# Gated MLP behind attention and a soft mixture: four plain turns become six Strassen turns, and float64 weights are made float32 in three operations in place of four

## The chip, the cores and the metric

The kernel runs on one core of one Trainium2 chip. The metric is the device time of one execution in microseconds. Each execution is the whole chain below, from the inputs in device memory to the output in device memory.

## The reference

Three layers follow each other. The first is a decayed linear attention over 4 batches, 8 heads, 768 positions and 64 channels. The second is a soft mixture of 8 experts with 4 slots each. The third, which the change is about, is a gated MLP over 3072 tokens:

```
h = x @ w_in                                  # x 3072x512, w_in 512x2048
g = h * (1.0 / (1.0 + np.exp(-1.702 * h)))
return (g @ w_out).astype(np.float32)         # w_out 2048x512
```

`w_in` and `w_out` reach the kernel as float64 (a float32 array times a numpy double). The kernel sees them as pairs of 32-bit words and has to put together the float32 value of each number itself, from the sign, exponent and upper mantissa in the upper word and three mantissa bits in the lower one.

## The kernel before

**Stages.** In order of time: attention in 32 steps (some 0 to 143 us), the experts, whose weights stream in through the SP queue (to 184 us), a short passage in which the slot outputs are turned into the matrix `W2s`, and then the MLP. In the MLP the output of the mixture is not written out: `h` comes straight from `W2s` and the transposed token weights `cT` with one product of depth 128.

**Plain turns.** The tokens are cut into four groups of 768 (`tg`), the 2048 hidden columns into 16 blocks of 128 (`f`). A plain turn `j` is one pair (`tg`, `f`): `do_h(j)` makes the 768 values of `g` for the block (`h_mm`, two products of 384 columns, then `h_gate` on ScalarE), splits them into a rounded upper part `GHI` (`h_hi`, ScalarE) and a rest `GLO` (`h_lo`, VectorE), and `do_out(j)` runs 18 products of 128x512: six blocks of 128 tokens, each as GHI with whi, GHI with wlo, GLO with whi. The work `do_h(j)` is issued in the middle of turn `j-2`, in front of its tenth product. One group (`WHOLE = 2`) goes through all 16 blocks in plain turns. The other three go through the first few only: `HF` = 4 blocks, and for the last of them `LAST_HF` = 8.

**Strassen turns.** What is left of the three groups is done in Strassen turns: 256 tokens against a pair of blocks (`p`, 256 hidden columns), with seven products in place of eight. A turn is 21 products of 128x256 and the two of 256 columns that make `h` (`s_h`). There are nine groups of such turns, one for each 256 tokens; their results are put together on VectorE (`ev_a` to `ev_d`) during the next group's first turns, and added to the rows in device memory.

**The weights.** The 27 late pieces of the weights (15 rows of `w_out`, 12 pieces of `w_in`) are loaded during the plain turns into three buffers (`f64`, `NST`), converted, and split. `LATE_IN` and `LATE_OUT` say at which `do_h` a piece is converted, and at the next one a row of `w_out` is split into `whi` and `wlo` (`split_hi` on ScalarE, `split_lo` on VectorE). `ROUNDS` operations of a conversion stand ahead of `h_lo` on VectorE, the rest behind it. `w2_a`, `w2_b` and `w2_c` extend `W2s` by 512 columns three times; they stand in given turns of the plain part. For the Strassen turns `make_sums`, `make_his` and `make_lows` make the sums of weight blocks for pair `p` in the turn that `PAIR_AT` gives and the one after it. Ten smaller pieces (`EARLY`) are converted during attention, with their last two operations on GpSimd.

**Order.** The order on each engine is that of the program text; nothing is moved by a scheduler. Each engine's queue runs in order.

Of the kernel before, what the change touches and what calls it, by code (L numbers as in the profile page):

```python
# [17 lines left out]
def attention_moe_gelu_kernel(  # L18
# [38 lines left out]
    TG = 2 * HS  # L57
    HF = 4

    LATE_IN = {1: (2, 4, 5, 6), 2: (9, 11, 13, 14), 3: (15, 16, 17, 18)}  # L60
    LATE_OUT = {4: 7, 5: 8, 6: 10, 7: 12, 8: 19, 9: 20, 10: 21, 11: 22, 12: 24, 13: 25, 14: 27, 15: 28}
    PAIR_AT = {2: 18, 3: 21, 4: 24, 5: 26, 6: 28, 7: 29}
    LAST_HF = 8
    ROUNDS = 3
    NST = 3
    F64_MIN = 2.0 ** -15 * 1.125
    CB = 256

    const = ctx.enter_context(tc.tile_pool(name="const", bufs=1, side="left"))
# [116 lines left out]
    def conversion(key, out, guard):  # L186
# [13 lines left out]
        yield  # L200
        if guard is DVE:
            DVE.scalar_tensor_tensor(out=out, in0=m, scalar=F64_MIN, in1=a.bitcast(F32),
                                     op0=ALU.is_ge, op1=ALU.mult)
        else:
            POOL.tensor_scalar(out=m, in0=m, scalar1=F64_MIN, scalar2=None, op0=ALU.is_ge)
            POOL.tensor_tensor(out=out, in0=a.bitcast(F32), in1=m, op=ALU.mult)

    def by_turns(*work, rounds=9):

        work = list(work)  # L210
        while work and rounds:
            work = [w for w in work if next(w, 0) is None]
            rounds -= 1
        return work
# [17 lines left out]
    def do_early(c):  # L232
        o = EARLY[c][-1]
        convert_abs(("early", c), o)
        by_turns(conversion(("early", c), o, POOL))


    S_a = [attn.tile([P, P], F32, tag=f"sa{i}", name=f"sa{i}", bufs=1) for i in range(4)]
# [244 lines left out]
    with tc.manual_schedule():  # L483
# [299 lines left out]
        def convert_early(f):  # L783
            convert_abs(("out", f))
            wo[f] = wo_ring[f]
            return conversion(("out", f), wo[f], DVE)

        def split_hi(f):
            ACT.activation(out=whi[f], in_=wo[f], func=AF.Copy)
# [89 lines left out]
        def convert_late(j, rounds=9):  # L879
            work = []  # L880
            for key in turns.get(j, ()):
                if key[0] == "out":
                    o = wo[key[1]] = wo_ring[key[1] % 10]
                else:
                    o = w_in_sb[key[1]][:, key[2], :]
                if key not in magn:
                    convert_abs(key)
                work.append(conversion(key, o, DVE))
            return by_turns(*work, rounds=rounds)

        def finish_late(j, work):
# [149 lines left out]
        def w2_rest():  # L1041
# [2 lines left out]
            rest0[:] = convert_late(0, ROUNDS)  # L1044


        extra = {(0, 3): w2_rest, (0, 6): lambda: do_h(1), (0, 13): lambda: do_h(2),
                 (7, 4): lambda: w2_a(1, "xt"), (9, 4): lambda: w2_b(1, "xt"), (9, 8): lambda: w2_c(1),
                 (15, 4): lambda: w2_a(2, "xt"), (16, 4): lambda: w2_b(2, "xt"), (16, 8): lambda: w2_c(2),
                 (19, 4): lambda: w2_a(3, "xt"), (20, 4): lambda: w2_b(3, "xt"), (20, 8): lambda: w2_c(3)}  # L1050

        def both(x, y):
            return lambda: (x(), y())
# [255 lines left out]
        for j in range(NJ):  # L1309
            at = {n: work for (jj, n), work in extra.items() if jj == j}  # L1310
            if 0 < j < NJ - AHEAD:
                at[9] = lambda: ahead(j + AHEAD)
                if j in (9, 16, 20):

                    at[9], at[12] = lambda: h_mm(j + AHEAD, (1,)), at[9]
            do_out(j, at)
# [39 lines left out]
```

## Time and profile before

| | |
|---|---|
| time, median of 3 runs | 479.23 us (478.05 to 479.63) |
| profiled execution, its own time | 478.11 us |
| its span, first to last instruction | 476.1 us |
| granted TensorE clock, mean | 1.000 |
| TensorE busy | 465.3 us, 98% |
| VectorE busy | 375.5 us, 79% |
| ScalarE busy | 303.3 us, 64% |
| GpSimd busy | 76.5 us, 16% |

The span is 2.0 us shorter than the execution's own time. Busy shares are means over stages that differ. In the rows further down PE is TensorE's matmuls, PEld its weight loads, DVE VectorE, ACT ScalarE, POOL GpSimd, SPq the queue of SP that issues most transfers.

### The profile page before, as it was taken

The page shows a single profiled execution, that of the slowest core. Times are in us where ns is not written, and L with a number is a line of the kernel's source. Part 1 is how long each engine was busy: PE and PEld are TensorE (multiplying, and loading weights), DVE is VectorE, ACT ScalarE, POOL GpSimd, SP SyncE. Part 2 cuts the span into 40 slices and gives each one's busy share as a digit, 9 for nine tenths or more (in the row PEclk, how much of TensorE's full clock was granted, in tenths as well). Part 3 has the DMA queues.
Part 4 walks back from the last instruction along what each step waited for, and adds up shares of the span by engine and source line. Part 5 has one row for each costly group of instructions (what it writes and reads, how often), then busy time and mean ns, then how long its engine had stood idle before and what let it go on. Part 6 is the DMA issues. An engine that isn't in the chain of part 4 may idle for free.

```text
span 476.1 us, 10660 instructions
## 1 busy us (share of the span) xinstructions
PE 465.3 (98%) x3991; PEld 388.0 (81%) x3991; DVE 375.5 (79%) x903; ACT 303.3 (64%) x605; POOL 76.5 (16%) x125
## 2 busy tenths in 40 slices
PE   7999999999999999999999999999999999999996
PEld 4887887888876444787888778888899999999996
DVE  5777988988875344897787689998779989888885
ACT  5877777777854155876865877566665655655551
POOL 3534434434311100000000000000001111011101
PEclk9999999999999999999999999999999999999999
DMA  7999999999999996465643532100313332133024
GB/s 186 259 283 285 269 297 270 276 302 289 290 335 387 410 407 252 131 222 178 219 133 108 202 133 89 44 0 2 133 46 45 45 45 29 18 45 45 9 38 89
DMA packets 81796, 81.52 MB, mean 171 GB/s; under 512 B 54736, under 2 KB 63440, under 8 KB 81744
## 3 DMA queue, kind: packets, MB, share of 16 engines
q1 hardware_dynamic: 79296, 76.63, 51.3%
q0 software_dynamic: 2304, 4.20, 6.4%
q8 instruction: 32, 0.52, 0.5%
q14 instruction: 20, 0.16, 0.1%
q10 hardware_dynamic: 144, 0.00, 0.0%
HBM read 69.80 MB, written 11.01 MB: 170 GB/s over the span
## 4 chain that ended last, share of the span: by engine, by line
PE 81%; DMA 10%; DVE 5%; SPq 1%; ACT 1%; issue 1%; DVEq 0%; ACTq 0%
PE bo L1014 26%; PE bp L1180 24%; DMA w<-in_moe_w_dram 7%; PE bs L301 4%; PE bx L348 3%; PE bx L340 3%; DMA k<-in_k_dram 2%; PE bsh L1136 2%; PE bq L263 2%; PE bst L314 2%; PE bhh L967 2%; PE bt L359 2%; PE bk L265 2%; PE bl L369 1%; PE bp L441 1%; SPq L128 1%
## 5 line engine op out<-in xcount | busy, mean ns | idle before, releaser
L1014 PE MATMUL bo<-wlo,GHI 128*128 128x512 f32 x192 | 75.3, 395 | 0.1
L1150 ACT ACTIVATE GHI<-G_all 128x896 fp32r<-128x896 f32 x48 | 45.9, 955 | 46.1 <-DVE G_all L1143 45.9
L1014 PE MATMUL bo<-whi,GLO 128*128 128x512 f32 x192 | 75.1, 394 | 0.0
L1014 PE MATMUL bo<-whi,GHI 128*128 128x512 f32 x192 | 74.8, 393 | 0.1
L1143 DVE TENSOR_TENSOR G_all<-G_all 128x128 f32<-128x128 f32 x192 | 47.4, 288 | 18.5 <-ACT G_all L1139 15.9
L1210 POOL DMA_DIRECT2D out_dram<-f x16 | 14.3, 1048 | 279.5 <-DVE G_all L1143 264.9
L1180 PE MATMUL bp<-tc,GHI 128*128 128x256 f32 x288 | 55.9, 282 | 0.0
L1155 DVE TENSOR_TENSOR GLO<-G_all,GHI 128x896 fp32r<-128x896 f32 x48 | 52.1, 1085 | 0.0
L975 ACT ACTIVATE G_all<-bhh 128x384 f32<-128x384 f32 x64 | 28.2, 490 | 34.4 <-PE bhh L967 34.3
L1180 PE MATMUL bp<-whi,GHI 128*128 128x256 f32 x192 | 49.5, 281 | 0.0
L1180 PE MATMUL bp<-wlo,GHI 128*128 128x256 f32 x192 | 49.2, 282 | 0.0
L1180 PE MATMUL bp<-whi,GLO 128*128 128x256 f32 x168 | 47.5, 283 | 0.0
L1180 PEld LDWEIGHTS bp<-tc,GHI 128*128 128x128 f32 x288 | 44.4, 190 | 0.0
L1014 PEld LDWEIGHTS bo<-wlo,GHI 128*128 128x128 f32 x192 | 36.0, 188 | 9.6 <-issue 2.5
L1014 PEld LDWEIGHTS bo<-whi,GLO 128*128 128x128 f32 x192 | 36.0, 188 | 7.8 <-DVE GLO L981 0.3
L1014 PEld LDWEIGHTS bo<-whi,GHI 128*128 128x128 f32 x192 | 36.1, 188 | 7.5 <-DVE W2s L921 0.5
L1180 PE MATMUL bp<-tc,GLO 128*128 128x256 f32 x144 | 40.4, 280 | 0.0
L981 DVE TENSOR_TENSOR GLO<-G_all,GHI 128x768 fp32r<-128x768 f32 x32 | 30.6, 955 | 10.4 <-ACT GHI L978 10.2
L282 POOL TENSOR_TENSOR qdT<-qT,qtab 128x384 f32<-128x384 f32 x32 | 32.4, 1012 | 39.7 <-PE bx L340 16.7
L273 ACT ACTIVATE qT<-bq 128x384 f32<-128x384 f32 x32 | 22.6, 707 | 20.1 <-PE bq L263 18.4
L1180 PEld LDWEIGHTS bp<-wlo,GHI 128*128 128x128 f32 x192 | 34.7, 189 | 0.0
L1180 PEld LDWEIGHTS bp<-whi,GHI 128*128 128x128 f32 x192 | 34.6, 189 | 0.0
(231 smaller groups left out, 1040.2 us busy)
## 6 DMA issues: line engine op xcount, KB each, us to landing
w<-in_moe_w_dram SPq DMA_DIRECT2D x64, 512.0 KB, 6.7
f<-in_moe_w_out_dram SPq DMA_DIRECT2D x15, 512.0 KB, 3.3
qr<-in_q_dram SPq DMA_DIRECT2D x32, 192.0 KB, 4.2
k<-in_k_dram SPq DMA_DIRECT2D x64, 96.0 KB, 4.8
v<-in_v_dram SPq DMA_DIRECT2D x64, 96.0 KB, 4.1
f<-in_moe_w_in_dram SPq DMA_DIRECT2D x12, 512.0 KB, 3.8
out_dram<-o SPq DMA_DIRECT2D x24, 256.0 KB, 2.3
out_dram<-f POOLq DMA_DIRECT2D x16, 256.0 KB, 4.7
```

The lines of the kernel that those rows point to most:

```text
L273: ACT.activation(out=t.rearrange("m (p c) -> m c p", c=R), in_=bq[:, :HS].rearrange("m (c p) -> m c p", c=R), func=AF.Copy)
L282: POOL.tensor_tensor(out=qdT[s], in0=qT[s].rearrange("m (c i) -> m c i", c=R), in1=qtab[:, hp, None, :].to_broadcast([P, R, P]), op=ALU.mult)
L301: PE.matmul(bs[h][:, cs], kT[s][hs, cs], qT[s][hs, cs], start=True, stop=True)
L340: PE.matmul(bx[:, c * P:(c + 1) * P], state(s, first + c), qdT[s][:, c, :], start=(c == chunks[0]), stop=False)
L975: ACT.activation(out=g[j][:, u * HS:(u + 1) * HS], in_=bh[j][u][:, :HS], func=AF.Gelu_apprx_sigmoid)
L981: DVE.tensor_tensor(out=glo[j][:, o], in0=g[j][:, o], in1=ghi[j][:, o].bitcast(F32), op=ALU.subtract)
L1014: PE.matmul(ob[t], a[j][:, t * P:(t + 1) * P], w[f], start=(begin and i == 0), stop=(end and i == 2))
L1143: DVE.tensor_tensor(out=o, in0=x, in1=y, op=op)
L1150: ACT.activation(out=sh[j], in_=gs(j)[:, P:], func=AF.Copy)
L1155: DVE.tensor_tensor(out=sl[j], in0=gs(j)[:, P:], in1=sh[j].bitcast(F32), op=ALU.subtract)
L1180: PE.matmul(bank_of(gi, i)[1], x, w, start=begin, stop=end)
L1210: POOL.dma_start(out=rows_of(gi, k), in_=cells[:, C11 + 2 * k:C11 + 2 * k + 2], accum_op=ALU.add)
```

## The change

`LAST_HF` goes from 8 to 4, so that the last group, too, leaves plain turns after four blocks: 28 plain turns and 54 Strassen turns in place of 32 and 48. The tables that place the conversions, the sums and the `w2_` steps are written anew for 28 turns. A conversion loses its fourth operation, the guard that made tiny numbers zero. ScalarE, which took the absolute value of the upper word as it is, now multiplies it by 2^-112 as well, which puts the exponent in float32's place and lets tiny numbers become zero there; VectorE's first operation shifts ScalarE's result in place of the raw word. For the early pieces both GpSimd operations go.

```
-    LATE_OUT = {4: 7, 5: 8, 6: 10, 7: 12, 8: 19, 9: 20, 10: 21, 11: 22, 12: 24, 13: 25, 14: 27, 15: 28}
+    LATE_OUT = {4: 8, 5: 10, 6: 11, 7: 13, 8: 16, 9: 17, 10: 18, 11: 20, 12: 21, 13: 22, 14: 23, 15: 24}
...
-    LAST_HF = 8
-    ROUNDS = 3
+    LAST_HF = 4
+    ROUNDS = 2
...
-        ACT.activation(out=m, in_=staged[key][:, :, 1].bitcast(F32), func=AF.Abs)
+        ACT.activation(out=m, in_=staged[key][:, :, 1].bitcast(F32), func=AF.Abs, scale=F64_TO_32)
...
-        a = out.bitcast(U32) if key[0] != "early" else stage[key[1] % 2][:, 2 * CB:3 * CB]
-        DVE.tensor_scalar(out=a, in0=up, scalar1=3, scalar2=0x3FFFFFFF,
-                          op0=ALU.logical_shift_left, op1=ALU.bitwise_and)
+        a = m.bitcast(U32)
+        DVE.tensor_scalar(out=a, in0=a, scalar1=3, scalar2=None, op0=ALU.logical_shift_left)
         yield
-        DVE.scalar_tensor_tensor(out=a, in0=up, scalar=0xC0000000, in1=a,
+        DVE.scalar_tensor_tensor(out=a, in0=up, scalar=0x80000000, in1=a,
                                  op0=ALU.bitwise_and, op1=ALU.bitwise_or)
         yield
-        DVE.scalar_tensor_tensor(out=a, in0=low, scalar=29, in1=a,
+        DVE.scalar_tensor_tensor(out=out.bitcast(U32), in0=low, scalar=29, in1=a,
                                  op0=ALU.logical_shift_right, op1=ALU.bitwise_or)
-        yield
-        if guard is DVE:
-            DVE.scalar_tensor_tensor(out=out, in0=m, scalar=F64_MIN, in1=a.bitcast(F32),
-                                     op0=ALU.is_ge, op1=ALU.mult)
-        else:
-            POOL.tensor_scalar(out=m, in0=m, scalar1=F64_MIN, scalar2=None, op0=ALU.is_ge)
-            POOL.tensor_tensor(out=out, in0=a.bitcast(F32), in1=m, op=ALU.mult)
```

The rows below are the order of instructions on VectorE, line and operation, output from input, and size. First the passage from the experts to the MLP, in the kernel before; `wor` is a row of `w_out`, `f` the buffer with its float64, `cvm` ScalarE's absolute value, `W2s` the correction of the first columns of `W2s`, `wlo` a `split_lo`.

```order
L912 COPY soT<-bso 128x128 x2
L192 TENSOR_SCALAR wor_3153<-f_3156 128x512
L195 SCALAR_TENSOR_TENSOR wor_3153<-f_3156,wor_3153 128x512
L921 TENSOR_TENSOR W2s<-bw,W2s 64x128
L198 SCALAR_TENSOR_TENSOR wor_3153<-f_3156,wor_3153 128x512
L202 SCALAR_TENSOR_TENSOR wor_3153<-cvm,wor_3153 128x512
L921 TENSOR_TENSOR W2s<-bw,W2s 64x128
L792 TENSOR_TENSOR wlo_3302<-wor_3153,whi_3287 128x512
L981 TENSOR_TENSOR GLO<-G_all,GHI 128x768
```

The same place in the changed kernel:

```order
L905 COPY soT<-bso 128x128 x2
L193 TENSOR_SCALAR cvm<-cvm 128x512
L195 SCALAR_TENSOR_TENSOR cvm<-f_3136,cvm 128x512
L914 TENSOR_TENSOR W2s<-bw,W2s 64x128
L198 SCALAR_TENSOR_TENSOR wor_3133<-f_3136,cvm 128x512
L914 TENSOR_TENSOR W2s<-bw,W2s 64x128
L785 TENSOR_TENSOR wlo_3282<-wor_3133,whi_3267 128x512
L974 TENSOR_TENSOR GLO<-G_all,GHI 128x768
```

The two operations ahead of the first `W2s` row now read `cvm`, where they read the float64 buffer, and the row L202 is gone.

The second place is the turn in which the sums for the first pair (`sp`, `wos`) are made. Before, this is turn 18, with one conversion in it:

```order
L1095 TENSOR_TENSOR sp<-sp 128x256
L1095 TENSOR_TENSOR sp<-wos_3321,sp 128x256
L1095 TENSOR_TENSOR wos_3321<-wos_3321,sp 128x256
L1095 TENSOR_TENSOR wos_3321<-wos_3321 128x256
L192 TENSOR_SCALAR wos_3325<-f_3156 128x512
L195 SCALAR_TENSOR_TENSOR wos_3325<-f_3156,wos_3325 128x512
L198 SCALAR_TENSOR_TENSOR wos_3325<-f_3156,wos_3325 128x512
L981 TENSOR_TENSOR GLO<-G_all,GHI 128x768
L792 TENSOR_TENSOR wlo_3309<-wos_3324,whi_3294 128x512
L202 SCALAR_TENSOR_TENSOR wos_3325<-cvm,wos_3325 128x512
```

In the changed kernel it is turn 15:

```order
L1089 TENSOR_TENSOR sp<-sp 128x256
L1089 TENSOR_TENSOR sp<-wos_3301,sp 128x256
L1089 TENSOR_TENSOR wos_3301<-wos_3301,sp 128x256
L1089 TENSOR_TENSOR wos_3301<-wos_3301 128x256
L193 TENSOR_SCALAR cvm<-cvm 128x512 x2
L195 SCALAR_TENSOR_TENSOR cvm<-f_3136,cvm 128x512 x2
L974 TENSOR_TENSOR GLO<-G_all,GHI 128x768
L785 TENSOR_TENSOR wlo_3289<-wos_3304,whi_3274 128x512
L198 SCALAR_TENSOR_TENSOR wos_3305<-f_3136,cvm 128x512
L198 SCALAR_TENSOR_TENSOR w_in_3313<-f_3136,cvm 128x512
```

Two conversions stand there now, two operations of each ahead of `GLO` and one of each behind it.

## Rows read from the trace of the kernel before

**Rows 1.** Busy time by stage: stretch, length, PE, PEld, DVE, ACT, POOL, clock, DMA share.

```profile
core 0: us, PE busy (x) PEld busy (x) DVE busy (x) ACT busy (x) POOL busy (x), PEclk, DMA share, GB/s
20.00:184.00 164.00, 160.84 (x2001) 118.66 (x1997) 118.71 (x360) 108.62 (x266) 52.31 (x74) 1.00 1.02 318
206.00:330.00 124.00, 124.00 (x561) 99.98 (x560) 104.46 (x179) 85.75 (x164) 0.00 (x0) 1.00 0.37 124
345.00:462.00 117.00, 117.00 (x988) 117.00 (x987) 100.82 (x245) 67.47 (x95) 12.50 (x14) 1.00 0.25 38
```

**Rows 2.** Timeline of PE, the products `h_mm` (start, duration, engine, line).

```profile
221.33 0.51 PE L967 MATMUL bhh<-cT,W2s 128*128 128x384 f32 x2
...
227.03 0.51 PE L967 MATMUL bhh<-cT,W2s 128*128 128x384 f32 x2
...
241.08 0.51 PE L967 MATMUL bhh<-cT,W2s 128*128 128x384 f32 x2
...
307.34 0.51 PE L967 MATMUL bhh<-cT,W2s 128*128 128x384 f32 x2
...
329.77 0.51 PE L967 MATMUL bhh<-cT,W2s 128*128 128x384 f32 x2
```

**Rows 3.** The chain that ended last, Strassen turns, the first and last of 44.

```profile
342.55 2.50 PE bp L1180 x21
...
459.99 2.51 PE bp L1180 x21
```

**Rows 4.** Timeline of DVE, passage to the MLP (idle time before an instruction in brackets).

```profile
187.16 0.43 DVE L192 TENSOR_SCALAR wor<-f 128x512 uint32<-128x512 uint32 x1
187.62 0.69 DVE L195 SCALAR_TENSOR_TENSOR wor<-f,wor 128x512 uint32<-128x512 uint32 x1
188.46 0.29 DVE L921 TENSOR_TENSOR W2s<-bw,W2s 64x128 fp32r<-64x128 f32 x1
```

**Rows 5.** Timeline of ACT, the same place.

```profile
187.35 0.69 ACT L183 ACTIVATE cvm<-f 128x512 f32<-128x512 f32 x1
```

**Rows 6.** Timeline of PE, the same place.

```profile
188.81 0.62 PE L967 MATMUL bhh<-cT,W2s 128*128 128x384 f32 x2
189.26 1.89 PE L926 MATMUL bw<-w_in,soT 128*128 128x256 f32 x8
190.80 1.52 PE L1014 MATMUL bo<-whi,GHI 128*128 128x512 f32 x5
```

**Rows 7.** Timeline of PEld, turns 1 and 2.

```profile
196.68 0.19 PEld L1014 LDWEIGHTS bo<-whi,GLO 128*128 128x128 f32 x1 [0.27 <-DVE GLO L981]
...
201.34 0.19 PEld L1014 LDWEIGHTS bo<-wlo,GHI 128*128 128x128 f32 x1 [0.53 <-DVE wlo L792]
```

**Rows 8.** Timeline of DVE in the later plain turns.

```profile
290.50 0.76 DVE L921 TENSOR_TENSOR W2s<-w2raw,W2s 64x128 fp32r<-64x128 f32 x2
...
295.17 0.42 DVE L1095 TENSOR_TENSOR wos<-wos 128x256 f32<-128x256 f32 x1
...
296.88 0.95 DVE L981 TENSOR_TENSOR GLO<-G_all,GHI 128x768 fp32r<-128x768 f32 x1
297.75 0.68 DVE L792 TENSOR_TENSOR wlo<-wor,whi 128x512 fp32r<-128x512 f32 x1
298.35 0.75 DVE L1105 TENSOR_TENSOR whi<-wos,whi 128x256 fp32r<-128x256 f32 x2
...
299.69 0.42 DVE L192 TENSOR_SCALAR wor<-f 128x512 uint32<-128x512 uint32 x1
...
301.49 0.95 DVE L981 TENSOR_TENSOR GLO<-G_all,GHI 128x768 fp32r<-128x768 f32 x1
...
309.50 0.96 DVE L981 TENSOR_TENSOR GLO<-G_all,GHI 128x768 fp32r<-128x768 f32 x1 [0.60 <-ACT GHI L978]
```

**Rows 9.** Timeline, an early conversion: DVE's first operation, and ACT's.

```profile
28.47 0.29 DVE L192 TENSOR_SCALAR stage<-stage 128x256 uint32<-128x256 uint32 x1
...
29.53 0.43 ACT L183 ACTIVATE w_in<-stage 128x256 f32<-128x256 f32 x1
```

**Rows 10.** Waits of SP's queue: line, releaser, us in total, times, longest.

```profile
SPq L229 <- DVE stage L198: 1.7, 3, 0.9
```

More of the change, by code (lines that the diff above doesn't have):

```diff
@@ L58, in attention_moe_gelu_kernel @@
     HF = 4
-    LATE_IN = {1: (2, 4, 5, 6), 2: (9, 11, 13, 14), 3: (15, 16, 17, 18)}
-    LATE_OUT = {4: 7, 5: 8, 6: 10, 7: 12, 8: 19, 9: 20, 10: 21, 11: 22, 12: 24, 13: 25, 14: 27, 15: 28}
-    PAIR_AT = {2: 18, 3: 21, 4: 24, 5: 26, 6: 28, 7: 29}
-    LAST_HF = 8
-    ROUNDS = 3
+    LATE_IN = {1: (2, 4, 5, 6), 2: (7, 9, 11, 12), 3: (14, 15, 17, 19)}
+    LATE_OUT = {4: 8, 5: 10, 6: 11, 7: 13, 8: 16, 9: 17, 10: 18, 11: 20, 12: 21, 13: 22, 14: 23, 15: 24}
+    W2_AT = {1: (9, 11), 2: (14, 16), 3: (19, 21)}
+    PAIR_AT = {2: 15, 3: 17, 4: 19, 5: 21, 6: 23, 7: 25}
+    LAST_HF = 4
+    ROUNDS = 2
     NST = 3
-    F64_MIN = 2.0 ** -15 * 1.125
+    F64_TO_32 = 2.0 ** -112
     CB = 256
@@ L182, in convert_abs, with conversion @@
         m = mask
-        ACT.activation(out=m, in_=staged[key][:, :, 1].bitcast(F32), func=AF.Abs)
+        ACT.activation(out=m, in_=staged[key][:, :, 1].bitcast(F32), func=AF.Abs, scale=F64_TO_32)
         magn[key] = m
-    def conversion(key, out, guard):
+    def conversion(key, out):
         t, m = staged.pop(key), magn.pop(key)
         up, low = t[:, :, 1], t[:, :, 0]
-        a = out.bitcast(U32) if key[0] != "early" else stage[key[1] % 2][:, 2 * CB:3 * CB]
-        DVE.tensor_scalar(out=a, in0=up, scalar1=3, scalar2=0x3FFFFFFF,
-                          op0=ALU.logical_shift_left, op1=ALU.bitwise_and)
+        a = m.bitcast(U32)
+        DVE.tensor_scalar(out=a, in0=a, scalar1=3, scalar2=None, op0=ALU.logical_shift_left)
         yield
-        DVE.scalar_tensor_tensor(out=a, in0=up, scalar=0xC0000000, in1=a,
+        DVE.scalar_tensor_tensor(out=a, in0=up, scalar=0x80000000, in1=a,
                                  op0=ALU.bitwise_and, op1=ALU.bitwise_or)
         yield
-        DVE.scalar_tensor_tensor(out=a, in0=low, scalar=29, in1=a,
+        DVE.scalar_tensor_tensor(out=out.bitcast(U32), in0=low, scalar=29, in1=a,
                                  op0=ALU.logical_shift_right, op1=ALU.bitwise_or)
-        yield
-        if guard is DVE:
-            DVE.scalar_tensor_tensor(out=out, in0=m, scalar=F64_MIN, in1=a.bitcast(F32),
-                                     op0=ALU.is_ge, op1=ALU.mult)
-        else:
-            POOL.tensor_scalar(out=m, in0=m, scalar1=F64_MIN, scalar2=None, op0=ALU.is_ge)
-            POOL.tensor_tensor(out=out, in0=a.bitcast(F32), in1=m, op=ALU.mult)
     def by_turns(*work, rounds=9):
@@ L234, in do_early @@
         convert_abs(("early", c), o)
-        by_turns(conversion(("early", c), o, POOL))
+        by_turns(conversion(("early", c), o))
     S_a = [attn.tile([P, P], F32, tag=f"sa{i}", name=f"sa{i}", bufs=1) for i in range(4)]
@@ L785, in convert_early @@
             wo[f] = wo_ring[f]
-            return conversion(("out", f), wo[f], DVE)
+            return conversion(("out", f), wo[f])
         def split_hi(f):
@@ L887, in convert_late @@
                     convert_abs(key)
-                work.append(conversion(key, o, DVE))
+                work.append(conversion(key, o))
             return by_turns(*work, rounds=rounds)
@@ L1044, in w2_rest @@
             rest0[:] = convert_late(0, ROUNDS)
[L1047 to L1050, printed above, removed]
+        extra = {(0, 3): w2_rest, (0, 6): lambda: do_h(1), (0, 13): lambda: do_h(2)}
+        for n, (ja, jb) in W2_AT.items():
+            extra[ja, 4] = lambda n=n: w2_a(n, "xt")
+            extra[jb, 4] = lambda n=n: w2_b(n, "xt")
+            extra[jb, 8] = lambda n=n: w2_c(n)
         def both(x, y):
@@ L1312, in attention_moe_gelu_kernel @@
                 at[9] = lambda: ahead(j + AHEAD)
-                if j in (9, 16, 20):
+                if j in [jb for ja, jb in W2_AT.values()]:
                     at[9], at[12] = lambda: h_mm(j + AHEAD, (1,)), at[9]
```

## The prediction

> **What bounds the kernel now.** I read the busy time by stage first, then the timeline of TensorE's products, then the waits. From 20 to 184 us the transfers are the limit: the DMA share is 1.02 of a possible 1, with VectorE and GpSimd far from full [rows 1]. TensorE shows as busy there too, but a product that waits for its weights counts as busy, so that figure alone decides nothing. From 206 us on it is the other way round: the DMA share falls to 0.37 and 0.25, and TensorE is busy for 124.00 of 124.00 us and for 117.00 of 117.00 us, at a granted clock of 1.00, the higher level of 2.4 GHz [rows 1]. The reader should see that these two stretches are regular as well as full: plain turns follow each other at one distance, Strassen turns at another [rows 2, 3]. So in the MLP time is TensorE's turns. The only places where another engine holds it are the passage into the MLP and turns 1 and 2 [rows 6, 7].
>
> **The exchange of turns.** The products `h_mm` at 307.34 and 329.77 are five plain turns apart: 22.43 / 5 = 4.486 us a turn [rows 2]. The four turns that go are the last group's blocks 4 to 7, ordinary ones, so 4 x 4.486 = 17.94 us go. The first and the last of the 44 Strassen turns on the chain are 43 turns apart: 117.44 / 43 = 2.731 us a turn, evictions of the group before included [rows 3]. Six more cost 16.39 us. The exchange gives **-1.55 us**. The bounds are narrow, 0.2 us either way, because both distances are those of turns in which nothing but TensorE was late. VectorE has 100.82 us of work in 117.00 us there [rows 1], and the new groups of six turns leave it more room for the same evictions than groups of four did.
>
> A rule can be set beside this. The Trainium skill, "TensorE: Matmul & The Clock Gate", section "Back-to-back issue gap", lists 518 cycles for 512 columns and 262 for 256 at 2.4 GHz. With 390 for 384 columns, my estimate from that page's pattern, a plain turn would be 18 x 518 + 2 x 390 = 10,104 cycles or 4.21 us, a Strassen turn 23 x 262 = 6,026 cycles or 2.51 us, and the exchange -1.77 us. The trace has both turns longer, by 0.28 and 0.22 us, so the measured -1.55 stands in the sum.
>
> **The first conversion of the MLP.** Before, VectorE's first two operations on row 1 of `w_out` began at 187.16 straight from the raw words and were out of the way when the correction of `W2s` was due at 188.46 [rows 4]. Now they need ScalarE's `cvm`, which runs from 187.35 and ends at 188.04 [rows 5]. Queued behind them on VectorE is that correction, and TensorE waits for it: `h_mm(0)` starts at 188.81, right behind it, then the 256-column piece of `W2s`, and only then the first product of turn 0 at 190.80 [rows 6]. The two operations take 0.46 (187.16 to 187.62) and at most 0.69 us, so the correction starts at 188.04 + 0.46 + 0.69 = 189.19 in place of 188.46. That is **+0.7 us** for everything behind it. The bounds are 0 (if ScalarE got to `cvm` earlier than the row says) and 0.75.
>
> **What the shorter conversions give back.** In turns 1 and 2 weight loads sat idle 0.27 us for `GLO` and 0.53 us for a `wlo` [rows 7]. Each of these stands behind conversions on VectorE. One operation of 0.69 us less ahead of the first, and two less ahead of the second, outweigh the 0.7 us by which all of it starts later, so both waits should go. A weight load runs ahead of its product, so TensorE lost less than these 0.80 us. I take half, **-0.4 us**, with bounds 0 and -0.8.
>
> **VectorE in turns 15 to 22.** Here the change packs work closer, and this is the edit I cost at nothing that needs its cover named. In these eight turns stand nine conversions, eight `GLO`, seven `split_lo`, four sets of sums, four of lows, one `w2_a` and two corrections of `W2s`. By distances between starts [rows 8]: three operations of a conversion 1.80 (299.69 to 301.49), `GLO` 0.87, a split 0.60, sums 1.71, lows 1.34; the `w2_a` operation as a split 0.60; a pair of corrections 0.76. The sum is 16.2 + 7.0 + 4.2 + 6.8 + 5.4 + 0.6 + 1.5 = 41.7 us. TensorE needs 8 x 4.486 = 35.9 us for the turns, and 1.21 more for `w2_a` (221.33 to 227.03) and some 0.6 each for two `w2_b` (227.03 to 241.08 less three turns) [rows 2]: 38.3 us. VectorE falls 3.4 us behind. What covers it is the lead of two turns: `GLO` can start 2.16 us after `h_mm` (307.34 to 309.50 [rows 2, 8]), and is wanted at the third product two turns later, 2 x 4.486 - 7 x 0.23 = 7.36 us after `h_mm`, with 0.23 from 4.486 less a pair of `h_mm` over 18. Less its own 0.87 that leaves 4.3 us. 3.4 is inside, so **0**, with the upper bound under the second rival. ScalarE has 85.75 us of work in 124.00 us [rows 1], and its part of a conversion stays one operation. I know no row of an absolute value with a scale; I take it at the 0.69 us of the row without.
>
> **Attention.** Twenty GpSimd operations go. Nothing limits there but transfers, and no byte of them changes, so **0**. Two bounds. In two of the ten early conversions VectorE came first: at 28.47, where ScalarE's part ended only at 29.96 [rows 9]. VectorE must now wait 1.5 us with the next step's masks behind it; twice, and passed on in full, this is +3.0. On the other side SP's queue was held 1.7 us by conversions [rows 10]; all of it gone is -1.7.
>
> **The sum** is -1.55 + 0.7 - 0.4 = -1.25 us: a span of 476.1 - 1.25 = 474.85 and an own time of 478.11 - 1.25 = 476.9. The profiled execution is 1.1 us below the median of the three runs, so against the median I forecast 479.23 - 1.25 = **478.0 us**. A measurement of this kernel can tell about 0.3%, or 1.4 us, from no change.
>
> **The rivals.**
>
> *The front gets shorter.* If SP issues loads earlier and the stream of expert weights ends earlier by the whole 1.7 us, and turns 1 and 2 give back the full 0.8, the sum is -1.55 + 0.7 - 0.8 - 1.7 = -3.35: 475.9. For it speaks that the loads are the limit to 184 us; against it that the DMA share is already full, so that an earlier issue only queues. Chance 0.12.
>
> *VectorE falls further behind than its lead.* The place is `GLO` in turns 17 to 24. If VectorE's operations don't overlap but each costs its full duration [rows 4, 8], the eight turns hold nine conversions of 1.81, `GLO` of 0.96, splits of 0.68, and sums and lows of four operations at 0.42: 16.3 + 7.7 + 4.8 + 6.8 + 6.7 + 0.7 + 1.5 = 44.5 us, 6.2 behind, against 4.3 of lead. TensorE would wait 1.9 us, and the sum is +0.65: 479.9, slower than before. It decides once VectorE is 5.6 us behind, 2.2 more than I count, over some 60 operations 37 ns each. Against it speaks that a split starts 0.87 us after a `GLO` that lasts 0.95 [rows 8]. Chance 0.13.
>
> The Trainium skill, "VectorE: DVE Perf Modes", section "The DRAIN you can't avoid", says that the next operation does not start until the pipe is empty, and refers to a later section for those that start earlier. By that alone this rival would be the forecast, at 479.9; the row of the split just named does not agree with it.
>
> *Early conversions are paid for.* If half of the 3.0 us of waits in attention reaches the end, the sum is +0.25: 479.5. Against it speaks that the stage waits for transfers anyway, so a late step catches up. Chance 0.10.
>
> **How the numbers follow.** My forecast, TensorE as the limit with the passage 0.7 later, has 0.60 and its own range 477.2 to 478.8, from the bounds of the exchange and of the first turns. The remaining 0.05 is for what I don't see. Faster by over 0.3% means below 477.8: four tenths of the forecast, all of the first rival and a little of the rest, 0.38. Slower by over 0.3% means above 480.7, which needs the second rival at more than its price or both the second and third, 0.13. The same: 0.49. The range that holds 8 in 10 runs from 476.2 to 479.8: it takes in the forecast, the third rival and part of both others.
>
> **What would show it.** In the changed profile, starts of `h_mm` 4.49 us apart from turn 3 to the end of the plain part and Strassen turns 2.73 apart would show the exchange. VectorE idle until about 188.1 (if the experts end where they did) with ScalarE's `cvm` as releaser, and the first product of turn 0 some 0.7 us further from the last expert product, would show the passage. Weight loads in turns 1 and 2 without a wait for `GLO` or `wlo` would show the gain. Any wait of a weight load for `GLO` from turn 15 on, or plain turns longer than 4.5 us there, would show the second rival. What makes me wrong most easily is the front: the passage into the MLP begins where the expert weights have arrived, and if that moves by half a microsecond, my sum is off by as much.

## The result, and the profile after

The changed kernel takes 481.92 us (median of 7 runs, 480.18 to 483.74) beside 479.13 us for the kernel before (7 runs, 477.56 to 479.63): a ratio of 1.007, 95% interval 1.0051 to 1.009. It is slower, by more than a measurement of this kernel needs to tell. The forecast was 478.0 us, its range 476.2 to 479.8.

The profiled execution took 481.92 us, with a span of 479.9. Its busy time by stage answers to [rows 1]; the columns are those of that group. The plain turns now end at 327.53 (first `bp` product), so the second and third stretch are cut anew.

```profile
core 0: us, PE busy (x) PEld busy (x) DVE busy (x) ACT busy (x) POOL busy (x), PEclk, DMA share, GB/s
20.00:184.00 164.00, 161.41 (x2003) 117.97 (x1997) 117.24 (x360) 107.87 (x265) 36.11 (x54) 1.00 1.03 320
206.00:326.00 120.00, 117.97 (x523) 93.34 (x523) 89.65 (x169) 86.21 (x166) 0.00 (x0) 0.99 0.40 127
328.00:462.00 134.00, 133.36 (x1123) 133.16 (x1122) 111.89 (x273) 75.56 (x107) 12.43 (x14) 1.00 0.24 41
```

TensorE is no longer full in the plain part: 117.97 of 120.00 us, at a mean granted clock of 0.99. Elsewhere the two kinds of turns are what they were. The timeline of TensorE late in the plain part, as in [rows 2], has two turns in 311.74 - 302.76 = 8.98 us, 4.49 each:

```profile
302.76 0.51 PE L960 MATMUL bhh<-cT,W2s 128*128 128x384 f32 x2
...
311.74 0.51 PE L960 MATMUL bhh<-cT,W2s 128*128 128x384 f32 x2
```

The chain that ended last, as in [rows 3], has 47 distances of Strassen turns in 128.40 us, 2.732 each:

```profile
335.38 2.50 PE bp L1174 x21
...
463.78 2.51 PE bp L1174 x21
```

The span can be cut at four starts that every run here has in the timeline of TensorE: the experts' first warm-up product (`bwarm`, 185.36 before, 184.51 after), the first `bo`, the first `bp`, and the end.

| us | before | after | difference |
|---|---|---|---|
| up to the first warm-up product | 185.36 | 184.51 | -0.85 |
| from there to the first `bo` | 5.44 | 6.21 | +0.77 |
| first `bo` to first `bp` (plain turns) | 150.28 | 136.81 | -13.47 |
| first `bp` to the end (Strassen turns) | 135.02 | 152.37 | +17.35 |
| span | 476.1 | 479.9 | +3.8 |

By the prediction the plain part should have lost 17.94 + 0.4 = 18.34 us and the Strassen part gained 16.39. So 4.87 us are missing in the one and 0.96 are too many in the other. Of the first, 0.6 is in turn 4, behind the evictions of the first group (5.13 us from one `h_mm` to the next, where the mended kernel further down has 4.53), and 3.99 in one place, the turns in which the last short group's six outputs are evicted; most of the rest is in turns 8 to 10, behind a wait of `cvm` for another load. The timeline of all engines there has these rows (in brackets the idle time before an instruction, and what ended it):

```profile
242.31 3.46 SPq L175 DMA_DIRECT2D f<-in_moe_w_in_dram  x2
...
245.32 0.67 ACT L184 ACTIVATE cvm<-f 128x512 f32<-128x512 f32 x1 [1.74 <-DMA f<-in_moe_w_out_dram]
245.89 0.59 ACT L1013 ACTIVATE o<-bo 128x512 f32<-128x512 f32 x1
...
246.50 4.93 SPq L1014 DMA_DIRECT2D out_dram<-o  x4
...
248.10 0.59 ACT L1013 ACTIVATE o<-bo 128x512 f32<-128x512 f32 x1
...
250.48 0.60 ACT L1013 ACTIVATE o<-bo 128x512 f32<-128x512 f32 x1 [1.78 <-DMA out_dram<-o]
...
251.89 0.62 PE L960 MATMUL bhh<-cT,W2s 128*128 128x384 f32 x2 [0.95 <-ACT G_all L968]
...
253.81 0.61 PE L1007 MATMUL bo<-whi,GHI 128*128 128x512 f32 x1 [0.61 <-ACT o L1013]
```

ScalarE first waits 1.74 us for a weight load, then, three evictions later, 1.78 us for a store: all three buffers of the outputs' tile `o` are still being written to device memory. The gates `G_all` stand behind that eviction in ScalarE's queue, and TensorE waits for the gates and for the next eviction. Taken over the plain part, the stores also land later. In the DMA issues of 200 to 330 us (queue, count, size, median us to landing), before:

```profile
out_dram<-o SPq DMA_DIRECT2D x18, 256.0 KB, 2.9
```

and after:

```profile
out_dram<-o SPq DMA_DIRECT2D x23, 256.0 KB, 4.5
```

The median hides the groups: the six stores of the last short group have 3.5 us before (issues of 240 to 285 us) and 3.6 after. So the late landing does not by itself make the wait; the part on the step that failed comes back to this.

In this execution the pause has a second price. In the busy time of three stretches around it (columns as above) TensorE sits idle for 1.56 us from 250 to 254, and in the four microseconds after that the granted clock is 0.57, which is the lower level of 1.2 GHz for most of them:

```profile
240.00:250.00 10.00, 9.93 (x44) 7.91 (x43) 7.30 (x13) 5.58 (x11) 0.00 (x0) 1.00 0.62 207
250.00:254.00 4.00, 2.44 (x11) 1.43 (x10) 1.25 (x2) 3.49 (x7) 0.00 (x0) 1.00 0.38 144
254.00:258.00 4.00, 4.00 (x11) 3.13 (x12) 3.42 (x6) 2.95 (x6) 0.00 (x0) 0.57 0.65 173
```

At the full level these last four microseconds would have held 4 x (1 - 0.57) = 1.7 us more work. The missing time of the Strassen part stands at its beginning, and has the same kind of releaser: VectorE's eviction waits for a store, the `GLO` behind it is late, and TensorE waits for that (timelines of VectorE and TensorE):

```profile
331.37 0.69 DVE L1019 COPY o<-bo 128x512 f32<-128x512 f32 x1 [2.02 <-DMA out_dram<-o]
...
334.04 0.39 PE L1174 MATMUL bp<-whi,GLO 128*128 128x256 f32 x1 [0.64 <-DVE GLO L1149]
```

### The profile page after: what moved, and what is told of

Read it like the earlier page. It is cut to its first block, busy times and chain, and to the rows that moved or that the text cites. A ratio compares the mean times of both kernels' runs of the same rounds, so it can differ in the third digit from the quotient of the medians.

```text
span 479.9 us, 10778 instructions
## 1 busy us (share of the span) xinstructions
PE 466.6 (97%) x4049; PEld 389.6 (81%) x4049; DVE 363.3 (76%) x902; ACT 304.2 (63%) x605; POOL 60.4 (13%) x105
## 4 chain that ended last, share of the span: by engine, by line
PE 72%; DMA 16%; ACT 4%; DVE 3%; issue 2%; SPq 2%; ACTq 0%; DVEq 0%
PE bp L1174 26%; PE bo L1007 20%; DMA w<-in_moe_w_dram 8%; DMA k<-in_k_dram 4%; PE bs L294 4%; PE bx L341 3%; PE bx L333 3%; PE bsh L1130 3%; PE bq L256 2%; PE bst L307 2%; DMA out_dram<-o 2%; PE bt L352 2%; PE bk L258 2%; PE bhh L960 2%; SPq L129 1%
## 5 line engine op out<-in xcount | busy, mean ns | idle before, releaser
L1007 PE MATMUL bo<-whi,GHI 128*128 128x512 f32 x168 | 66.2, 398 | 1.0 <-ACT o L1013 0.9
L1007 PE MATMUL bo<-wlo,GHI 128*128 128x512 f32 x168 | 66.5, 399 | 0.0
L1007 PE MATMUL bo<-whi,GLO 128*128 128x512 f32 x168 | 66.1, 397 | 0.0
L1174 PE MATMUL bp<-whi,GHI 128*128 128x256 f32 x234 | 59.1, 281 | 0.0
L1174 PE MATMUL bp<-wlo,GHI 128*128 128x256 f32 x234 | 58.6, 282 | 0.0
L1149 DVE TENSOR_TENSOR GLO<-G_all,GHI 128x896 fp32r<-128x896 f32 x54 | 58.6, 1085 | 0.0
L1174 PE MATMUL bp<-whi,GLO 128*128 128x256 f32 x198 | 56.1, 283 | 0.6 <-DVE GLO L1149 0.6
L1174 PEld LDWEIGHTS bp<-wlo,GHI 128*128 128x128 f32 x234 | 41.8, 190 | 0.0
L1174 PEld LDWEIGHTS bp<-whi,GHI 128*128 128x128 f32 x234 | 41.7, 189 | 0.0
L1174 PEld LDWEIGHTS bp<-whi,GLO 128*128 128x128 f32 x198 | 37.5, 189 | 0.8 <-DVE GLO L1149 0.8
```

The costliest lines, as they stand in the source:

```text
L1007: PE.matmul(ob[t], a[j][:, t * P:(t + 1) * P], w[f], start=(begin and i == 0), stop=(end and i == 2))
L1149: DVE.tensor_tensor(out=sl[j], in0=gs(j)[:, P:], in1=sh[j].bitcast(F32), op=ALU.subtract)
L1174: PE.matmul(bank_of(gi, i)[1], x, w, start=begin, stop=end)
```

## The experiments

Two theories stood at the start. A: an eviction waits for one of three `o` buffers whose store has not landed, and this stalls TensorE. B: ScalarE is held by `cvm`, whose weight load is issued too late. What the expectations call the stall of turn 11 begins with the evictions of turn 11 and reaches into turns 12 and 13. Each edit is against the changed kernel where nothing else is said, and every kernel does the whole computation. Cuts of an edit are marked `...`; where it changes the number of buffers or the engine that issues the stores, the same is done at the second such place of the kernel, which is left out here.

**Four buffers for `o`.**

```
-            o = mp.tile([P, DM], F32, tag="o", name="o", bufs=3)
+            o = mp.tile([P, DM], F32, tag="o", name="o", bufs=4)
```

> The changed kernel with four output buffers `o` in place of three, nothing else. Theory A (an eviction on ScalarE or VectorE stands and waits for an output buffer whose store has not landed, and everything behind it on that engine is late): the waits of `o` for its stores in plain turns 11 and 27 go (1.78 and 2.02 us), with them the low-clock stretch at 254 to 258 us, and the time falls from 481.9 to about 478.5 us. Theory B (ScalarE is held by `cvm`, which waits for a weight load that was issued too late): only what is not behind `cvm` goes, at most 1.0 us at the start of the Strassen turns: about 481.

Measured: 478.11 us (475.79 to 481.26), ratio to before 0.9997 (0.9975 to 1.0019). The stall is gone, though ScalarE still waits for the load, as its timeline shows:

```profile
244.59 0.67 ACT L184 ACTIVATE cvm<-f 128x512 f32<-128x512 f32 x1 [1.56 <-DMA f<-in_moe_w_out_dram]
```

A wait of that length for a load alone costs TensorE little there (0.32 us, in the table further down), so B by itself falls.

**Loads earlier.** Three operations of a conversion ahead of `GLO`, so that a float64 buffer comes free sooner.

```
-    ROUNDS = 2
+    ROUNDS = 3
```

> The changed kernel with all three operations of a conversion ahead of `GLO` (ROUNDS = 3), so that a float64 buffer is free, and the next load issued, some 1.4 us earlier; `GLO` comes 0.6 to 1.2 us later. Theory B: the wait of `cvm` of 1.74 us at 245 us goes, the evictions behind it start 1.7 us earlier, and the time falls to about 479. Theory A: the store that turn 11 waits for is still 4 us on its way, so most of the loss stays: about 481.5.

Measured: 478.45 us (476.11 to 479.94), ratio 0.9996 (0.9979 to 1.0014). By its own expectation A falls here too: the wait for the load is gone, a wait for a store is left, and TensorE hardly feels it. ScalarE's timeline:

```profile
247.12 0.60 ACT L1013 ACTIVATE o<-bo 128x512 f32<-128x512 f32 x1 [1.34 <-DMA out_dram<-o]
```

**The exchange of turns alone,** with the conversion in four operations.

```
-    ROUNDS = 2
+    ROUNDS = 3
...
-        ACT.activation(out=m, in_=staged[key][:, :, 1].bitcast(F32), func=AF.Abs, scale=F64_TO_32)
+        ACT.activation(out=m, in_=staged[key][:, :, 1].bitcast(F32), func=AF.Abs)
...
-        DVE.tensor_scalar(out=a, in0=a, scalar1=3, scalar2=None, op0=ALU.logical_shift_left)
+        DVE.tensor_scalar(out=a, in0=up, scalar1=3, scalar2=0x3FFFFFFF,
+                          op0=ALU.logical_shift_left, op1=ALU.bitwise_and)
...
+        if guard is DVE:
+            DVE.scalar_tensor_tensor(out=out, in0=m, scalar=F64_MIN, in1=a.bitcast(F32),
+                                     op0=ALU.is_ge, op1=ALU.mult)
...
```

> 28 and 54 turns with the new tables, but the conversion of four operations with its guard and three rounds ahead of `GLO`. Theory A (tables and turns bring the loss): 482 us or more, with the waits of turn 11 as in the changed kernel; the passage into the MLP as before, 5.4 us from the first warm-up product to the first product of turn 0. Theory B (the conversion's order brings the loss): about 478.5, the exchange of turns alone. VectorE falling behind (my second rival, with 2.4 us a conversion) would add waits of products for `GLO` in turns 16 to 23, some 2 us more.

Measured: 486.49 us (485.37 to 487.88), ratio 1.0172 (1.0149 to 1.0195). There is no wait for a load near the stall, and one wait for a store:

```profile
250.16 0.60 ACT L1021 ACTIVATE o<-bo 128x512 f32<-128x512 f32 x1 [3.05 <-DMA out_dram<-o]
```

And in the weight loads' waits of 260 to 345 us (us in total, times, longest) stands what the second rival foresaw, VectorE behind with `GLO`:

```profile
PEld bo L1015 <- DVE GLO L982: 3.3, 6, 1.2
```

With three operations this row is absent. So the shorter conversion is what lets 28 plain turns hold the same conversions.

**The shorter conversion alone,** with the tables of before, and still two operations of a conversion ahead of `GLO`.

```
-    LATE_OUT = {4: 8, 5: 10, 6: 11, 7: 13, 8: 16, 9: 17, 10: 18, 11: 20, 12: 21, 13: 22, 14: 23, 15: 24}
+    LATE_OUT = {4: 7, 5: 8, 6: 10, 7: 12, 8: 19, 9: 20, 10: 21, 11: 22, 12: 24, 13: 25, 14: 27, 15: 28}
...
-    LAST_HF = 4
+    LAST_HF = 8
...
```

> 32 and 48 turns with the old tables, but the conversion of three operations (two rounds ahead of `GLO`). Theory A: only the passage (+0.7) and the first turns (-0.5) change: 479.1 to 479.6 us. Theory B: loads are issued later here too, and ScalarE waits for them: 480.5 or more.

Measured: 478.09 us (476.08 to 480.38), ratio 0.9995 (0.9975 to 1.0015). From the first warm-up product to the first `bo` it takes 6.20 us, as after, and behind that no part moves by more than 0.6 us. ScalarE waits for no load here, against theory B, though its stores land as late as after: 4.3 us at the median (DMA issues of 195 to 330 us). The slower time thus needs the exchange of turns.

**Four buffers, early loads, and the passage mended.** The first conversion's two operations of VectorE go behind the correction of `W2s`.

```
-    ROUNDS = 2
+    ROUNDS = 3
...
-        next(second)
-        next(second)
...
-            o = mp.tile([P, DM], F32, tag="o", name="o", bufs=3)
+            o = mp.tile([P, DM], F32, tag="o", name="o", bufs=4)
...
+        next(second)
+        next(second)
```

> The kernel after with four buffers for the outputs' tile `o`, weight loads one round of the list earlier, and the first conversion's two VectorE operations of the MLP put behind the correction of W2s again. Theory A (evictions wait for one of the output buffers whose store hasn't landed): the stall in turn 11 is gone, the distance from the first bo product to the first bp product is about 131.9 us as the exchange of turns gave it, the passage is back at 5.45 us, and the time is 475 to 476.5 us beside a kernel before at about 478.5. Theory B (ScalarE held by a conversion whose weight load was issued late): the same for the stall, since the loads are early too; then no more than 0.3 us is left of any wait for cvm in turns 3 to 15. If both were wrong and the low clock came by itself, 478 to 479.

Measured: 475.51 us (474.06 to 478.63) beside 478.0, ratio 0.9954 (0.9934 to 0.9974): faster than both kernels. The busy time shows TensorE full in both stretches again:

```profile
206.00:320.00 114.00, 114.00 (x518) 91.73 (x517) 89.93 (x169) 85.10 (x165) 0.00 (x0) 1.00 0.39 131
321.00:460.00 139.00, 139.00 (x1173) 139.00 (x1171) 117.64 (x287) 79.51 (x110) 12.42 (x14) 1.00 0.23 39
```

From the first `bo` (188.55) to the first `bp` (320.53) it is 131.98 us, and 151.47 from there to the end; the prediction's terms give 150.28 - 18.34 = 131.94 and 135.02 + 16.39 = 151.41.

**`w2_a` and `w2_b` one turn earlier.**

```
-    W2_AT = {1: (9, 11), 2: (14, 16), 3: (19, 21)}
+    W2_AT = {1: (8, 10), 2: (14, 16), 3: (19, 21)}
```

> The kernel after with only the two pieces w2_a and w2_b of group 1's down weights one turn earlier (8 and 10 in place of 9 and 11), so that w2_b no longer stands in the turn that evicts the last short group's outputs. Theory A (output buffers and their stores): the evictions of turn 11 still meet three buffers and the same loads, so a wait for a store of 1 to 2 us stays; one product group less stands in that turn, so TensorE's pause there is shorter by at most the 0.6 us of w2_b, 480 to 482 us. Rival (the placing of w2_b in the output turn is what stalls, not the buffers): turn 11 lasts 4.6 us, no stretch at the lower clock follows, 478 us.

Measured: 480.59 us (477.57 to 481.82), ratio 1.005 (1.003 to 1.0069). Where `w2_b` stands is not the cause: the wait for a store stays, in front of one eviction and at 2.79 us longer than expected, while no load holds ScalarE for more than 0.41 us from turn 10 to 13:

```profile
254.19 1.84 ACT L1013 ACTIVATE o<-bo 128x512 f32<-128x512 f32 x3 [2.79 <-DMA out_dram<-o]
```

**The passage alone.**

```
-        next(second)
-        next(second)
...
+        next(second)
+        next(second)
```

> The kernel after with only the first conversion of the MLP moved: its two VectorE operations stand behind the correction of W2s. By the prediction's step on the passage: from the experts' first warm-up product to the first bo product 5.44 to 5.5 us in place of 6.21, everything behind it 0.7 us earlier, and the stall of turn 11 as it was (both theories): 481 us. If the 0.77 us had another cause (ScalarE's own position, for one), the distance stays at 6.2 us.

Measured: 478.68 us (476.81 to 480.88), ratio 1.0022 (1.0002 to 1.0042). The mechanism holds: from the first warm-up product (183.54) to the first `bo` (188.97) it is 5.43 us. The time came out 2.3 us lower than expected, and in the profiled execution the stall was milder too. ScalarE's two waits are there, but together 3.29 us, and the granted clock stays at 1.00:

```profile
244.38 0.66 ACT L184 ACTIVATE cvm<-f 128x512 f32<-128x512 f32 x1 [2.48 <-DMA f<-in_moe_w_out_dram]
...
248.56 0.60 ACT L1011 ACTIVATE o<-bo 128x512 f32<-128x512 f32 x1 [0.81 <-DMA out_dram<-o]
```

**The kernel before with two buffers.**

```
-            o = mp.tile([P, DM], F32, tag="o", name="o", bufs=3)
+            o = mp.tile([P, DM], F32, tag="o", name="o", bufs=2)
```

> The kernel before with two buffers for the outputs' tile `o` in place of three, nothing else changed. Theory A (a store that hasn't landed holds the next eviction, that holds ScalarE or VectorE, and TensorE pauses): the kernel before falls into the same stall that the change brought, in the turns that evict a group of more than two outputs: DMA out<-o as releaser of the evictions, and 3 us or more in all over the kernel before. Theory B (a conversion waiting for its load): nothing of the loads changes, so the time is that of before within 1 us.

Measured: 490.45 us (489.56 to 492.71), ratio 1.028 (1.0247 to 1.0312). The store's wait is made in a kernel that did not have it. ScalarE's first such wait, and the stretch behind it, in which the lower clock shows as well:

```profile
212.98 0.60 ACT L1020 ACTIVATE o<-bo 128x512 f32<-128x512 f32 x1 [4.06 <-DMA out_dram<-o]
```

```profile
213.00:216.00 3.00, 1.32 (x5) 0.86 (x5) 0.75 (x1) 2.97 (x6) 0.00 (x0) 1.00 0.52 158
216.00:219.00 3.00, 2.69 (x6) 1.83 (x6) 2.53 (x5) 1.31 (x4) 0.00 (x0) 0.51 0.76 285
```

**Stores issued by GpSimd.**

```
-                SP.dma_start(out=out[r0:r0 + P, :], in_=o)
+                POOL.dma_start(out=out[r0:r0 + P, :], in_=o)
```

> The kernel after with the 24 stores of output rows issued by GpSimd, which has nothing else to do there, in place of SP; loads stay with SP. If a store lands late because it stands behind 512-KB weight loads in SP's own queue (theory A with that cause), stores land in 2 to 3 us at the median in place of 4.5, the evictions' waits for out<-o are below 0.5 us, turn 11 lasts 4.5 us, and the time is 477.5 to 478.5 us. If they are late because the DMA engines themselves share their time between loads and stores, landing stays at 4 us or more and the time at 480.5 to 482. Theory B (cvm) expects no change of the stall from it.

Measured: 480.41 us (479.22 to 482.5), ratio 1.0054 (1.0027 to 1.0081). A queue of their own does not make the stores land sooner; in the DMA issues of 195 to 330 us the median is 4.4 us:

```profile
out_dram<-o POOLq DMA_DIRECT2D x22, 256.0 KB, 4.4
```

**Half of the evictions by VectorE.**

```
-                ACT.activation(out=o, in_=ob[t], func=AF.Copy)
+                if t % 2:
+                    DVE.tensor_copy(out=o, in_=ob[t])
+                else:
+                    ACT.activation(out=o, in_=ob[t], func=AF.Copy)
```

> The kernel after with every second eviction of the short groups done by VectorE in place of ScalarE; three buffers and the stores as before. If what makes the stall is that an eviction which waits for a buffer holds ScalarE's gates behind it, then half of the waits now hold VectorE's GLO instead, and turn 11 still has a pause of 1 to 3 us: 479.5 to 482 us. If ScalarE were simply too full in turn 11 (the rival: its work, not the wait), taking three evictions of 0.6 us from it ends the stall: 478 us.

Measured: 480.76 us (477.61 to 482.41), ratio 1.0048 (1.0023 to 1.0073). Three evictions less on ScalarE did not end the stall, so ScalarE was not simply too full. The pause has gone to VectorE's queue: from 195 to 330 us weight loads wait four times for its evictions (waits: us in total, times, longest). In VectorE's timeline one of these evictions starts 2.14 us late; what released it the profile does not name.

```profile
PEld bo L1007 <- DVE o L1014: 3.9, 4, 2.0
```

```profile
251.03 0.69 DVE L1014 COPY o<-bo 128x512 f32<-128x512 f32 x1 [2.14 <-issue]
```

**Stores issued by ScalarE.**

```
-                SP.dma_start(out=out[r0:r0 + P, :], in_=o)
+                ACT.dma_start(out=out[r0:r0 + P, :], in_=o)
```

> The kernel after with the 24 stores of output rows issued from ScalarE's own queue, each right behind its eviction, in place of SP. The same test as with GpSimd, with another issuing engine: by the queue as the cause, landing of 2 to 3 us and no wait for out<-o above 0.5 us, less what issuing costs ScalarE (its gates later by that much); 477.5 to 479 us. By the DMA engines' sharing as the cause, 480.5 to 482.5.

Measured: 488.24 us (486.83 to 489.44), ratio 1.0216 (1.0191 to 1.0242). Landing agrees with the expectation for shared engines. The time missed both. Each issue stands in ScalarE's queue: the first group's evictions begin 1.03 us apart (207.92 to 208.95 in its timeline) where the changed kernel has 0.68 (206.02 to 206.70), and the weight loads of `bo` now wait for evictions eight times. How much of the some 6 us over the changed kernel comes from that was not told apart. DMA issues, then waits, of 195 to 330 us:

```profile
out_dram<-o ACTq DMA_DIRECT2D x19, 256.0 KB, 4.3
```

```profile
PEld bo L1007 <- ACT o L1013: 5.2, 8, 1.0
```

**Four buffers and later loads.** After the first runs a joint theory stood in the place of A and B: what counts is the sum of ScalarE's waits, since both stand in one queue.

```
-    ROUNDS = 2
+    ROUNDS = 1
...
-            o = mp.tile([P, DM], F32, tag="o", name="o", bufs=3)
+            o = mp.tile([P, DM], F32, tag="o", name="o", bufs=4)
```

> The kernel after with four buffers for the outputs' tile `o` (as in the first run of this study) and one operation of a conversion ahead of GLO in place of two, so that a float64 buffer comes free later and weight loads are issued later. No eviction should wait for a store; ScalarE's waits for a weight load (cvm) should grow from the 1.56 us of that run to 2 to 3 us around turns 10 to 12. Theory A (only the wait for a store stalls TensorE): no stall, the distances of h_mm in turns 11 to 13 as in the first run, 478 to 478.7 us. The joint theory (what counts is the sum of ScalarE's waits for stores and for loads there, since both stand in one queue; up to 1.6 us of them cost TensorE 0.3 to 0.6, 3.3 and 3.5 cost it 2.2 and 4.0): with 2 to 3 us of waits for loads alone TensorE loses 1 to 2.5 us around turn 12 or in other turns, 479 to 481 us.

Measured: 480.23 us (478.41 to 482.97), ratio 1.0029 (1.0008 to 1.005). There is no wait for a store in turns 10 to 13, a longer one for a load, and TensorE loses time all the same:

```profile
246.06 0.66 ACT L184 ACTIVATE cvm<-f 128x512 f32<-128x512 f32 x1 [2.88 <-DMA f<-in_moe_w_out_dram]
```

**The sum of the waits.** ScalarE's waits in that place and the time from `h_mm` in turn 10 to `h_mm` in turn 13, both from the timelines, the latter beside the 14.03 us (237.92 to 251.95) of the kernel that has no wait. Each row is one execution:

| kernel | wait for a load | wait for a store | turn 10 to 13 | lost |
|---|---|---|---|---|
| four buffers, early loads, passage | 0 | 0 | 14.03 | 0 |
| four buffers | 1.56 | 0 | 14.35 | 0.32 |
| loads earlier | 0 | 1.34 | 14.58 | 0.55 |
| four buffers, later loads | 2.88 | 0 | 15.68 | 1.65 |
| stores by GpSimd | 1.43 | 1.74 | 16.11 | 2.08 |
| passage alone | 2.48 | 0.81 | 16.21 | 2.18 |
| exchange alone | 0 | 3.05 | 17.88 | 3.85 |
| changed kernel | 1.74 | 1.78 | 18.02 | 3.99 |

Only the last two have a stretch at the lower clock behind the pause, of 1.7 us each by the method above (the exchange alone has 0.91, 0.50 and 0.74 in three stretches of 2 us). Less these, they lost 2.15 and 2.27. In every row, then, TensorE loses what ScalarE's waits have over some 0.8 to 1.25 us, whichever transfer they are for. The kernel with `w2_a` and `w2_b` earlier, whose turns differ, agrees: 2.79 us of wait, and 6.19 us from `h_mm` in turn 12 to the next, where the kernel without waits has 4.53, a loss of 1.66.

Turn 4 agrees too. ScalarE's eviction there waits in the kernel before, and `h_mm` is 4.53 us from the next:

```profile
211.88 1.85 ACT L1020 ACTIVATE o<-bo 128x512 f32<-128x512 f32 x3 [1.10 <-DMA out_dram<-o]
```

In the changed kernel it waits 0.61 us longer, and the distance is 5.13 us. The profile names a product as releaser, but the store whose buffer it needs, issued at 206.86, took 5.0 us:

```profile
211.90 1.87 ACT L1013 ACTIVATE o<-bo 128x512 f32<-128x512 f32 x3 [1.71 <-PE bo L1007]
```

## Why the prediction was wrong, point by point

**The exchange of turns** was right. In the kernel without waits both parts agree with its terms within 0.1 us (131.98 for 131.94, 151.47 for 151.41), and both turns have the distances of before. This again puts them above the figures that the Trainium skill, "TensorE: Matmul & The Clock Gate", section "Back-to-back issue gap", led to: 4.49 us measured where these gave 4.21, 2.732 where they gave 2.51.

**The first conversion of the MLP** was right, +0.77 for a forecast of +0.7. VectorE's two operations now wait for `cvm`, the correction is queued behind them, and `h_mm` of turn 0 waits for it. These are the timelines of VectorE, ScalarE and TensorE, which answer to [rows 4 to 6]:

```profile
187.19 0.43 DVE L193 TENSOR_SCALAR cvm<-cvm 128x512 uint32<-128x512 uint32 x1 [0.80 <-ACT cvm L184]
187.66 0.69 DVE L195 SCALAR_TENSOR_TENSOR cvm<-f,cvm 128x512 uint32<-128x512 uint32 x1
188.38 0.29 DVE L914 TENSOR_TENSOR W2s<-bw,W2s 64x128 fp32r<-64x128 f32 x1
```

```profile
186.50 0.67 ACT L184 ACTIVATE cvm<-f 128x512 f32<-128x512 f32 x1
```

```profile
188.73 0.61 PE L960 MATMUL bhh<-cT,W2s 128*128 128x384 f32 x2 [0.58 <-DVE W2s L914]
...
190.72 1.05 PE L1007 MATMUL bo<-whi,GHI 128*128 128x512 f32 x3
```

Moved behind the correction, the two operations cost nothing: 5.43 and 5.44 us in the two runs that do it.

**What the shorter conversions give back** was right. The waits of [rows 7] for `GLO` and `wlo` are gone, and from the first `bo` to `h_mm` in turn 2 it takes 11.98 us (190.72 to 202.70) where it took 12.49: -0.51 for a forecast of -0.4.

**VectorE in turns 15 to 22** was right as far as VectorE goes: the weight loads' waits from 260 us on name no `GLO` of plain turns, and a split still starts 0.87 us behind a `GLO` of 0.95, as in [rows 8]:

```profile
296.72 0.95 DVE L974 TENSOR_TENSOR GLO<-G_all,GHI 128x768 fp32r<-128x768 f32 x1
297.59 0.69 DVE L785 TENSOR_TENSOR wlo<-wor,whi 128x512 fp32r<-128x512 f32 x1
```

The second rival was real, but its place is the exchange without the shorter conversion.

**The step that failed** stands at the end of the same paragraph: "ScalarE has 85.75 us of work in 124.00 us [rows 1], and its part of a conversion stays one operation". The operation's price was right, 0.67 us. But ScalarE was costed by its busy share, as if its queue could not be held by a transfer, and the place looked at was turns 15 to 22, while the stall is in 11 to 13. The new tables move the last short group's outputs from turn 15 to turn 11, next to loads in pairs, and two operations ahead of `GLO` in place of three keep a float64 buffer longer, so that loads are issued later. The sum has no term for that: neither for the three buffers of `o`, nor for a load that an operation of ScalarE must wait for, nor for both in one queue. It measured +4.87 us in the plain part, of which 1.7 is the lower clock, and +0.96 at the start of the Strassen turns; the prediction had 0 for both.

The profile before had what a term needed, but not in its median. With three buffers the fourth eviction waits for the first one's store, so what counts is the time between the two in ScalarE's queue. In turn 11 of the changed kernel the first eviction ends at 246.48 and the third at about 248.70; a store may thus take 2.2 us before the fourth is late, and this one took 3.9. In turn 15 of the kernel before ScalarE's gates stand between the third and the fourth:

```profile
262.34 0.60 ACT L1020 ACTIVATE o<-bo 128x512 f32<-128x512 f32 x1 [0.64 <-PE bo L1014]
...
267.94 1.55 ACT L1020 ACTIVATE o<-bo 128x512 f32<-128x512 f32 x3
```

The first ends at 262.94 and the fourth starts at 267.94 without a wait, 5.0 us later. In turn 11 the gates come behind four evictions in place of three, because `w2_b` stands in that turn. With `w2_b` a turn earlier there are three again, yet the stores took 5 us and the wait stays. The median over all stores decides nothing: the shorter conversion alone has 4.3 us and is not slower, the exchange alone has 2.4 (DMA issues of 195 to 330 us) and waits 3.05. With two buffers the third eviction waits for the first store; in the first group they start 0.68 us apart, and even the fastest store of that run, 2.0 us, is too slow. Four buffers removed the wait in turns 11 to 13, though not each one elsewhere.

**Why the stores land late** is told by the queues. On GpSimd's queue or on ScalarE's they take 4.4 and 4.3 us, so it is not that they stand behind loads in SP's queue. The Trainium skill, "DMA: Bandwidth & Descriptors", section "Issuing engines are not separate DMA queues", says that transfers of all issuing engines run on the same 16 DMA engines and interleave; the landing times agree. When loads were issued earlier, the median fell to 2.5 us with nothing else changed, and with the tables of before and the later loads it is 4.3: the time at which loads are issued sets it, not the exchange of turns. In the changed kernel the store issued at 251.10, with no load in flight, took 2.0 us, and the one at 206.86, behind a load, 5.0. That loads in flight are all there is to it is not shown: at the start of the Strassen turns the store issued at 326.96 took 4.3 us with no weight load in flight, where before the same one took 2.3, and what held it stays open. What part of the 4.4 us is GpSimd's own way of issuing was not told apart.

**Attention** at 0 was right within what can be told. An early conversion did come to wait as feared (timelines of ScalarE and VectorE at the place of [rows 9]), and SP's queue gave no gain that the end shows:

```profile
29.00 0.42 ACT L184 ACTIVATE w_in<-stage 128x256 f32<-128x256 f32 x1
29.45 0.29 DVE L193 TENSOR_SCALAR w_in<-w_in 128x256 uint32<-128x256 uint32 x1 [1.20 <-ACT w_in L184]
```

The kernel with the shorter conversion alone has 6.20 - 5.44 = +0.76 in the passage and 149.74 - 150.28 = -0.54 in the plain turns, +0.2 us in all, and measured -0.2 us with an interval of about 1 us either way. So neither the first nor the third rival is seen; an effect of the front below 1 us stays open.

## What to carry to other kernels

Where a change moves evictions or loads to other turns, a busy share is no cover: for each in-order queue write down every wait that a transfer can end, add those that stand in the same turns, and compare the sum with the engine's lead over the one that needs it. For a tile with n buffers that is stored, eviction k + n waits for the store of eviction k: read from the order in the queue how long that store may take, turn by turn, and set it against the landing times of that place, not against a median over the kernel; here they grew where loads were issued just ahead of the stores. A dependence on another engine that a cheaper form brings in (here `cvm` ahead of the first shift) is best put behind whatever the limiting engine waits for in the same queue.

## What the runs showed of the hardware that had not been expected

Short pauses of TensorE can cost twice their length: after 1.56 us of idle time in 250 to 254 us the granted clock averaged 0.57 over the next four, and 0.51 in 216 to 219 us of the kernel with two buffers. They need not. The kernel with the stores by GpSimd has 1.52 us of idle time in four and keeps the higher level; what makes the difference these runs do not show.

```profile
252.00:256.00 4.00, 2.48 (x11) 1.48 (x10) 1.45 (x2) 3.69 (x8) 0.68 (x2) 1.00 0.39 147
256.00:260.00 4.00, 4.00 (x19) 3.31 (x18) 3.41 (x7) 3.17 (x8) 1.10 (x2) 1.00 0.71 193
```

The stream of expert weights ends between 183.05 and 187.00 us (first warm-up product) from one profiled execution to the next, with no order by kernel. That is more than the change itself moves, so the stages are compared by distances behind that product, and the kernels by medians of 4 to 12 runs.
